# Load order at the start, w_out in long rows, and sixteen small loads late in the queue of a decode kernel

## Chip, cores, metric

One core of one Trainium2 chip at a time. The metric is device time in microseconds (us) of the whole kernel. Smaller is better.

## The reference, cut to what matters

A decode step for four sequences with one token each: an attention block over a cache of 4096 positions and 32 heads, and a gMLP block, both on the normalised input, added to the input.

```python
def _A_ref(x, k_cache, v_cache, wq, wo):             # x (4,1,640), caches (4,32,4096,128)
    q = (x @ wq).reshape(B, Sq, H, Dh).transpose(0, 2, 1, 3)
    scores = einsum('bhqd,bhkd->bhqk', q, k_cache) * Dh ** -0.5
    o = einsum('bhqk,bhkd->bhqd', softmax(scores), v_cache)
    return o.transpose(0, 2, 1, 3).reshape(B, Sq, H * Dh) @ wo

def _B_ref(x, w_in, w_sp, b_sp, w_out):              # w_in (640,1728), w_out (864,640)
    z = gelu(x @ w_in)
    z1, z2 = z[..., :864], layernorm(z[..., 864:])
    g = einsum('ts,bsf->btf', w_sp, z2) + b_sp       # S is 1: one scalar each
    return (z1 * g) @ w_out

xn = layernorm(x)
return x + _A_ref(xn, ...) + _B_ref(xn, ...)
```

The two caches are 268 MB in bfloat16 and every byte is used once.

## The kernel before

All large loads are issued on the queue of SyncE (SP), in program order. The K and V tiles (4 MB each), the weights of the start and the last wo share a pool of five buffers. Cuts are marked.

```python
wg = kv_tile("w_gmlp")                                       # buffer 0
nc.sync.dma_start(out=w_in,  in_=B_w_in.rearrange("(p c) f -> p c f", c=DC))
nc.sync.dma_start(out=w_out[:, 0:FC-1, :], in_=B_w_out[0:nf, :].rearrange("(c p) n -> p c n", p=P))  # rows of 1280 bytes
nc.sync.dma_start(out=w_out[:FL, FC-1, :], in_=B_w_out[nf:Fh, :])
for i, (c0, c1) in enumerate(((0, 3), (3, DC))):             # wq, two loads, buffers 1 and 2
    nc.sync.dma_start(out=..., in_=wq_v[:, c0:c1, :])
nc.scalar.dma_start(out=x_bf, in_=x_flat)
nc.scalar.dma_start(out=sb_bf[:, 0:1], in_=B_w_sp....to_broadcast((P, 1)))   # one 2-byte scalar to 128 partitions
nc.scalar.dma_start(out=sb_bf[:, 1:2], in_=B_b_sp.to_broadcast((P, 1)))
# ... layer norm of x, constants, gMLP, then q ...

def load_unit(cache, key, u, cuts=(0, T)):                   # a K or V tile
    t_sb = kv_tile(f"{key}{u}")
    for t0, t1 in zip(cuts[:-1], cuts[1:]):
        nc.sync.dma_start(out=t_sb[:, t0*Dh:t1*Dh], in_=src[:, t0*Dh:t1*Dh])

def load_x():                                                # x again, for the residual: 8 rows of 640 bytes
    nc.sync.dma_start(out=x_res[0:32:4, :], in_=x_flat.rearrange("b (h n) -> (b h) n", h=NH))

# in the schedule: load_x stands behind V30; then come V31 in four pieces and wo_last in three
at(NCH * (NU - 2) + VD, load_x)
```

The framework sets the semaphores. The trace shows how it does so for loads: eight semaphores are used in turn by all loads of SP and of ScalarE (ACT), and a load waits until the load eight places before it has landed. I call that the rule of eight. A load has landed when its last byte is in place and its semaphore says so.

## Time and profile before

| | before |
|---|---|
| time, median of 3 | 670.08 us |
| profiled execution | 670.88 us, span 669.1 us |
| bytes moved | 282.65 MB at 422 GB/s |
| busiest compute engine | TensorE, 50% of the span |
| time from 38 to 600 us | 431 GB/s, DMA share 1.00 |

In the views by stretches, each line has the stretch, its length, then busy time and number of instructions of each engine, the granted TensorE clock, the mean busy share of the 16 DMA engines, and GB/s. In the timelines of the SP queue each line has the start, the length from the first issue to the last of that group, line and operation, output and input, and the count. The time a sequencer waits between issues of a group is inside the length.

### The profile page before, as it was taken

The page shows a single profiled execution, that of the slowest core. Times are in us where ns is not written, and L with a number is a line of the kernel's source. Part 1 is how long each engine was busy: PE and PEld are TensorE (multiplying, and loading weights), DVE is VectorE, ACT ScalarE, POOL GpSimd, SP SyncE. Part 2 cuts the span into 40 slices and gives each one's busy share as a digit, 9 for nine tenths or more (in the row PEclk, how much of TensorE's full clock was granted, in tenths as well). Part 3 has the DMA queues.
Part 4 walks back from the last instruction along what each step waited for, and adds up shares of the span by engine and source line. Part 5 has one row for each costly group of instructions (what it writes and reads, how often), then busy time and mean ns, then how long its engine had stood idle before and what let it go on. Part 6 is the DMA issues. An engine that isn't in the chain of part 4 may idle for free.

```text
span 669.1 us, 6401 instructions
## 1 busy us (share of the span) xinstructions
PE 335.7 (50%) x2781; PEld 139.1 (21%) x2781; DVE 319.5 (48%) x253; ACT 60.4 (9%) x184; POOL 8.9 (1%) x40
## 2 busy tenths in 40 slices
PE   0647463546543664337555364454753366433745
PEld 0511121122111221113121031111311122111323
DVE  4279853465533455542555534346543355543300
ACT  0200210012000210003000030001200021000300
POOL 0010000000000000000000000000000000000000
PEclk9997777778777787676766677866767878567676
DMA  8999999999999999999999999999999999999995
GB/s 313 439 424 428 436 433 428 425 436 431 426 435 430 428 434 439 424 428 434 427 429 433 432 427 434 426 427 441 428 431 430 431 427 432 433 433 426 435 418 230
DMA packets 12900, 282.65 MB, mean 422 GB/s; under 512 B 1621, under 2 KB 3017, under 8 KB 4169
## 3 DMA queue, kind: packets, MB, share of 16 engines
q1 hardware_dynamic: 12568, 282.25, 98.6%
q8 instruction: 21, 0.34, 0.2%
q10 hardware_dynamic: 304, 0.01, 0.0%
q14 instruction: 7, 0.05, 0.0%
HBM read 282.25 MB, written 0.01 MB: 422 GB/s over the span
## 4 chain that ended last, share of the span: by engine, by line
DMA 56%; PE 15%; issue 13%; DVE 12%; ACT 3%; ACTq 0%; DVEq 0%
DMA k<-in_A_k_cache_dram 50%; DVE kT L318 8%; PE O L422 6%; DMA wo_last<-in_A_wo_dram 5%; PE S L336 3%; ACT p L364 3%; PE misc L439 2%; DMA sb_bf<-in_B_b_sp_dram 2%; PE x L377 1%; DVE m L343 1%; DVE om L442 1%; PE misc L251 1%; PE misc L347 1%; ACT O_sb L430 0%; PE zT_ps L209 0%
## 5 line engine op out<-in xcount | busy, mean ns | idle before, releaser
L318 DVE STREAM_TRANSPOSE kT<-k 128x2048 f32<-128x2048 f32 x128 | 284.6, 2280 | 215.0 <-DMA k<-in_A_k_cache_dram 212.4
L336 PE MATMUL S<-kT,QZ 128*32 128x512 bf16 x1024 | 203.7, 538 | 257.6 <-DVE kT L318 255.2
L336 PEld LDWEIGHTS <-QZ 128*32 128x32 bf16 x1024 | 57.3, 115 | 399.1 <-issue 386.7
L422 PE MATMUL O<-v,Zb 128*32 128x512 bf16 x992 | 93.1, 467 | 9.0 <-DMA v<-in_A_v_cache_dram 9.0
L422 PEld LDWEIGHTS <-Zb 128*32 128x32 bf16 x992 | 42.1, 112 | 41.0 <-issue 26.2
L364 ACT ACTIVATE p<-S,negmax 128x1024 bf16<-128x1024 f32 x16 | 17.7, 1109 | 272.0 <-DVE negmax L358 272.0
L430 ACT COPY O_sb<-O 128x512 f32<-128x512 f32 x16 | 9.4, 585 | 240.6 <-PE O L422 240.6
L388 ACT COPY Zb<-x 32x128 bf16<-32x128 bf16 x128 | 27.3, 255 | 10.2 <-PE x L377 9.5
L377 PE MATMUL x<-IdP,p 128*128 128x128 bf16 x128 | 16.1, 305 | 18.9 <-ACT p L364 18.6
L442 DVE SCALAR_TENSOR_TENSOR om<-misc,rinv,MkH 16x512 bf16<-16x512 f32 x7 | 5.2, 739 | 37.8 <-PE misc L439 37.8
L439 PE MATMUL misc<-O_sb,SelG 128*16 128x128 f32 x112 | 16.9, 289 | 2.0 <-DVE rinv L398 1.5
L377 PEld LDWEIGHTS <-p 128*128 128x128 bf16 x128 | 12.0, 138 | 22.6 <-ACT p L364 22.6
L275 POOL COPY QZ<-q 32x16 bf16<-32x16 bf16 x32 | 7.9, 246 | 455.4 <-PE S L336 420.9
L439 PEld LDWEIGHTS misc<-O_sb,SelG 128*16 128x16 f32 x112 | 10.1, 99 | 7.9 <-ACT O_sb L430 2.4
L474 DVE TENSOR_TENSOR oL<-misc,rinv 128x8 bf16<-128x8 f32 (+1 forms) x2 | 0.3, 168 | 22.6 <-PE misc L472 22.6
L343 DVE TENSOR_REDUCE m<-S 128x1 f32<-128x512 f32 x8 | 5.5, 691 | 10.2 <-PE S L336 10.2
L147 PE MATMUL misc<-ident_bf,wq 4*128 4x4 bf16 x5 | 0.4, 178 | 18.9 <-DVE wq L143 18.9
L368 DVE TENSOR_TENSOR rowsum<-rs 128x1 f32<-128x1 f32 x8 | 1.2, 155 | 17.0 <-ACT p L364 17.0
L347 PE MATMUL misc<-dg,ones_f 128*128 128x128 f32 x16 | 3.9, 324 | 9.0 <-DVE dg L345 9.0
L364 ACT ACT_TABLE_LOAD x1 | 1.3, 1283 | 54.8 <-DVE negmax L358 54.8
L460 PE MATMUL proj<-wo,oT 128*4 128x320 bf16 x56 | 5.0, 298 | 1.9 <-DVE oT L453 1.9
L251 PE MATMUL misc<-xnT,wq 128*128 128x4 bf16 x160 | 4.7, 166 | 1.1 <-issue 0.8
(93 smaller groups left out, 75.9 us busy)
## 6 DMA issues: line engine op xcount, KB each, us to landing
k<-in_A_k_cache_dram SPq DMA_DIRECT2D x32, 4096.0 KB, 43.3
v<-in_A_v_cache_dram SPq DMA_DIRECT2D x31, 4096.0 KB, 41.1
wo<-in_A_wo_dram SPq DMA_DIRECT2D x7, 640.0 KB, 44.6
wq<-in_A_wq_dram SPq DMA_DIRECT2D x1, 3072.0 KB, 19.5
w_gmlp<-in_B_w_in_dram SPq DMA_DIRECT2D x1, 2160.0 KB, 9.3
wq<-in_A_wq_dram SPq DMA_DIRECT2D x1, 2048.0 KB
v<-in_A_v_cache_dram SPq DMA_DIRECT2D x1, 2048.0 KB
v<-in_A_v_cache_dram SPq DMA_DIRECT2D x1, 1024.0 KB, 38.4
```

The source lines that it names most:

```text
L251: nc.tensor.matmul(q_ps[:, h, :], lhsT=wq_t[c][:, h * Dh:(h + 1) * Dh], rhs=xnT[:, c, :], start=(c == 0), stop=(c == DC - 1))
L318: nc.vector.transpose(kT[:], kw[:, ch * n:(ch + 1) * n])
L336: nc.tensor.matmul(S_ps[32 * q:32 * q + 32, :, :], lhsT=qz[:, b, kw, w0:w0 + 32], rhs=kT[:, i, :, kw // 2, :, kw % 2], start=(b == 0 and c ...
L343: nc.vector.tensor_reduce(out=m1[:], in_=S_ps[:].rearrange("p k m -> p (k m)"), axis=AX.X, op=ALU.max)
L347: nc.tensor.matmul(mm[:], lhsT=ones_f[:], rhs=dg[:], start=True, stop=True)
L364: nc.scalar.activation(out=p_i[:], in_=S_ps[:, 8 * i:8 * i + 8, None, :].to_broadcast((P, 8, HG, M)), func=ACT.Exp, bias=negmax[:, 0:1], s ...
L377: nc.tensor.transpose(x[:, t, :], p_bf[t // 8][:, t % 8].rearrange("p h m -> p (h m)"), IdP[:])
L388: nc.scalar.copy(out=dst, in_=src[:, 2 * bb + b1])
L422: nc.tensor.matmul(O_ps[32 * q:32 * q + 32, :, :], lhsT=Zb[bb][:, w0:w0 + 32], rhs=vv[:, e // 16, e % 16, :, :], start=(b1 == 0 and e < 4) ...
L430: nc.scalar.copy(out=O_sb[:], in_=O_ps[:])
L439: nc.tensor.matmul(oh[:], lhsT=SelG[:, bb, c].rearrange("p h b -> p (h b)"), rhs=O_sb[:, c, :], start=(bb == 0 and c == 0), stop=(bb == 1 ...
L442: nc.vector.scalar_tensor_tensor(out=om[:], in0=oh[:, None, :].to_broadcast((G, HG, Dh)), scalar=state.pop(("rinv", g))[:, 0:1], in1=MkH[: ...
```

## The change

The intent: let q, which the first K tile needs, come first; let the gMLP weights follow with w_out in long rows; take the two scalar loads off the ACT queue. Sixteen small loads over 1 to 16 rows are issued behind `load_x`, into a tile that nothing reads.

```diff
-    (w_gmlp: w_in, w_out, w_out rest on nc.sync)        # first before, moved behind wq
     (wq, two loads on nc.sync; x on nc.scalar)
-    nc.scalar.dma_start(out=sb_bf[:, 0:1], in_=B_w_sp....to_broadcast((P, 1)))
-    nc.scalar.dma_start(out=sb_bf[:, 1:2], in_=B_b_sp.to_broadcast((P, 1)))
+    nc.gpsimd.dma_start(out=sb_bf[:, 0:1], in_=B_w_sp....to_broadcast((P, 1)))
+    nc.gpsimd.dma_start(out=sb_bf[:, 1:2], in_=B_b_sp.to_broadcast((P, 1)))
+    (w_gmlp here, with:)
-    ... in_=B_w_out[0:nf, :].rearrange("(c p) n -> p c n", p=P)
+    ... in_=B_w_out[0:nf, :].rearrange("(p c) n -> p c n", p=P)      # one row of 7680 bytes a partition
...
+    (q matmuls and q3, moved ahead of the gMLP)
-    nc.tensor.matmul(zT_ps[...], lhsT=w_in[:, c, f0:f0 + n], ...)
+    w = w_in[:, c, f0:f0 + nf].rearrange("p (f a) -> p a f", a=FC - 1)[:, fc, :]   # strided, to match w_out
-    nc.vector.tensor_copy(out=sb_f[:], in_=sb_bf[:])
+    nc.gpsimd.tensor_copy(out=sb_f[:], in_=sb_bf[:])
...
+    probe = const.tile([64, 264], BF16)
+    def load_probe():
+        c0 = 0
+        for k in range(1, 17):
+            n = 8 + k
+            nc.sync.dma_start(out=probe[0:4 * k:4, c0:c0 + n], in_=A_wo[0:k, 0:n])
+            c0 += n
...
-    at(NCH * (NU - 2) + VD, load_x)
+    at(NCH * (NU - 2) + VD, lambda: (load_x(), load_probe()))
```

More of the change, by code (lines that the diff above doesn't have):

```diff
@@ L90 @@
     out_flat = out.rearrange("b s d -> (b s) d")
-    wg = kv_tile("w_gmlp")
-    n_in = DC * F2
-    w_in = wg[:, 0:n_in].rearrange("p (c f) -> p c f", c=DC)
-    nc.sync.dma_start(out=w_in, in_=B_w_in.rearrange("(p c) f -> p c f", c=DC))
-    w_out = wg[:, n_in:n_in + FC * NOUT].rearrange("p (c n) -> p c n", c=FC)
-    nf = (FC - 1) * P
-    nc.sync.dma_start(out=w_out[:, 0:FC - 1, :], in_=B_w_out[0:nf, :].rearrange("(c p) n -> p c n", p=P))
-    nc.sync.dma_start(out=w_out[:FL, FC - 1, :], in_=B_w_out[nf:Fh, :])
     wq_v = A_wq.rearrange("(p c) n -> p c n", c=DC)
@@ L113 @@
     sb_bf = const.tile([P, 2], BF16)
-    nc.scalar.dma_start(out=sb_bf[:, 0:1], in_=B_w_sp.rearrange("a b -> (a b)").to_broadcast((P, 1)))
-    nc.scalar.dma_start(out=sb_bf[:, 1:2], in_=B_b_sp.to_broadcast((P, 1)))
+    nc.gpsimd.dma_start(out=sb_bf[:, 0:1], in_=B_w_sp.rearrange("a b -> (a b)").to_broadcast((P, 1)))
+    nc.gpsimd.dma_start(out=sb_bf[:, 1:2], in_=B_b_sp.to_broadcast((P, 1)))
     sb_f = const.tile([P, 2], F32)
+    wg = kv_tile("w_gmlp")
+    n_in = DC * F2
+    w_in = wg[:, 0:n_in].rearrange("p (c f) -> p c f", c=DC)
+    nc.sync.dma_start(out=w_in, in_=B_w_in.rearrange("(p c) f -> p c f", c=DC))
+    w_out = wg[:, n_in:n_in + FC * NOUT].rearrange("p (c n) -> p c n", c=FC)
+    nf = (FC - 1) * P
+    nc.sync.dma_start(out=w_out[:, 0:FC - 1, :], in_=B_w_out[0:nf, :].rearrange("(p c) n -> p c n", p=P))
+    nc.sync.dma_start(out=w_out[:FL, FC - 1, :], in_=B_w_out[nf:Fh, :])
     ident_bf = const.tile([P, P], BF16)
@@ L200 @@
     proj = ps_j.tile([64, 512], F32)
+    q_ps = misc_ps([P, H, B], F32)
+    for h in range(H):
+        for c in range(DC):
+            nc.tensor.matmul(q_ps[:, h, :], lhsT=wq_t[c][:, h * Dh:(h + 1) * Dh], rhs=xnT[:, c, :],
+                             start=(c == 0), stop=(c == DC - 1))
+    q_bf = const.tile([P, H * B], BF16)
+    nc.vector.tensor_copy(out=q_bf[:], in_=q_ps[:].rearrange("p h b -> p (h b)"))
+    q3_ps = misc_ps([P, 4, H * B], F32)
+    for kw in range(4):
+        nc.tensor.matmul(q3_ps[:, kw, :], lhsT=Pm[:, kw, :, :].rearrange("p a j -> p (a j)"), rhs=q_bf[:],
+                         start=True, stop=True)
+    q3 = const.tile([P, 4, H * B], BF16)
+    nc.vector.tensor_copy(out=q3[:], in_=q3_ps[:])
     zT_ps = ps_g.tile([P, 2, FC, B], F32)
@@ L206 @@
             n = P if fc < FC - 1 else FL
-            f0 = part * Fh + fc * P
+            f0 = part * Fh
             for c in range(DC):
-                nc.tensor.matmul(zT_ps[:n, part, fc, :], lhsT=w_in[:, c, f0:f0 + n],
+                if fc < FC - 1:
+                    w = w_in[:, c, f0:f0 + nf].rearrange("p (f a) -> p a f", a=FC - 1)[:, fc, :]
+                else:
+                    w = w_in[:, c, f0 + nf:f0 + Fh]
+                nc.tensor.matmul(zT_ps[:n, part, fc, :], lhsT=w,
                                  rhs=xnT[:, c, :], start=(c == 0), stop=(c == DC - 1))
@@ L245 @@
     nc.vector.tensor_tensor(out=uT[:, :, 0:B], in0=z1, in1=t1[:], op=ALU.mult)
-    q_ps = misc_ps([P, H, B], F32)
-    for h in range(H):
-        for c in range(DC):
-            nc.tensor.matmul(q_ps[:, h, :], lhsT=wq_t[c][:, h * Dh:(h + 1) * Dh], rhs=xnT[:, c, :],
-                             start=(c == 0), stop=(c == DC - 1))
-    q_bf = const.tile([P, H * B], BF16)
-    nc.vector.tensor_copy(out=q_bf[:], in_=q_ps[:].rearrange("p h b -> p (h b)"))
-    q3_ps = misc_ps([P, 4, H * B], F32)
-    for kw in range(4):
-        nc.tensor.matmul(q3_ps[:, kw, :], lhsT=Pm[:, kw, :, :].rearrange("p a j -> p (a j)"), rhs=q_bf[:],
-                         start=True, stop=True)
-    q3 = const.tile([P, 4, H * B], BF16)
-    nc.vector.tensor_copy(out=q3[:], in_=q3_ps[:])
     for fc in range(FC):
```

## The prediction

> **What bounds the kernel now.** I read the page first: the busy table, the slices, the chain of waits.
>
> ```profile
> PE 335.7 (50%) x2781; PEld 139.1 (21%) x2781; DVE 319.5 (48%) x253; ACT 60.4 (9%) x184; POOL 8.9 (1%) x40
> ...
> DMA  8999999999999999999999999999999999999995
> GB/s 313 439 424 428 436 433 428 425 436 431 426 435 430 428 434 439 424 428 434 427 429 433 432 427 434 426 427 441 428 431 430 431 427 432 433 433 426 435 418 230
> ...
> DMA 56%; PE 15%; issue 13%; DVE 12%; ACT 3%; ACTq 0%; DVEq 0%
> ```
>
> No compute engine is busy over half of the span, and the transfer engines are full in every slice but the first and the last. The kernel streams 282 MB, so the time is start + bytes at full rate + tail. The issues view says how deep the queue is:
>
> ```profile
> k<-in_A_k_cache_dram SPq DMA_DIRECT2D x32, 4096.0 KB, 43.3
> v<-in_A_v_cache_dram SPq DMA_DIRECT2D x31, 4096.0 KB, 41.1
> wo<-in_A_wo_dram SPq DMA_DIRECT2D x7, 640.0 KB, 44.6
> ```
>
> A 4 MB load lands 41 to 43 us after its issue, although it takes only 4.194 MB / 431 GB/s = 9.7 us to move. Four loads are queued ahead of it: the sequencer is always far ahead, and that margin is what must not be lost. Next, busy time by stretches (the last two columns are DMA share and GB/s):
>
> ```profile
> 2.00:3.00 1.00, 0.00 (x0) 0.00 (x0) 0.92 (x1) 0.01 (x1) 0.00 (x0) 1.00 0.21 69
> 3.00:7.00 4.00, 0.00 (x0) 0.00 (x0) 1.11 (x3) 1.27 (x1) 0.00 (x0) 1.00 0.99 397
> 7.00:11.00 4.00, 0.00 (x0) 0.00 (x0) 0.00 (x0) 0.00 (x0) 0.00 (x0) 1.00 0.72 236
> 11.00:25.00 14.00, 3.75 (x80) 3.48 (x80) 7.95 (x37) 3.43 (x6) 0.00 (x0) 1.00 1.06 436
> ...
> 37.90:600.00 562.10, 287.05 (x2114) 110.17 (x2116) 290.67 (x184) 48.27 (x154) 5.89 (x24) 0.73 1.00 431
> ```
>
> The steady rate is 431 GB/s. The only recoverable hole at the start is 7 to 11 us: 236 GB/s, while w_out (in 1280-byte rows) and the two broadcast scalars go through. Last, the timeline of the issuing queue at the end and the queue's own waits:
>
> ```profile
> 603.30 3.16 SPq L289 DMA_DIRECT2D v<-in_A_v_cache_dram  x2
> 606.52 0.78 SPq L307 DMA_DIRECT2D x_res<-in_A_x_dram  x1
> 622.75 2.59 SPq L289 DMA_DIRECT2D v<-in_A_v_cache_dram  x4
> 634.78 19.70 SPq L299 DMA_DIRECT2D wo_last<-in_A_wo_dram  x3
> ```
> ```profile
> SPq L299 <- DMA v<-in_A_v_cache_dram: 28.0, 3, 9.4
> ```
>
> The three wo_last loads are issued at 634.78, 644.43 and 654.15. They go to one buffer that is free from the start of that stretch, and yet the last two wait for V loads that they have nothing to do with. The records behind the view name the semaphore of each transfer: eight of them are used in turn over all SP and ACT loads, and a load waits until the load eight places earlier has landed. Eight before the third wo_last is V30, which landed at 654.14; eight before the second is V29, at 644.42. That rule costs nothing now. It decides this case.
>
> **What the Trainium skill says.** "DMA: Bandwidth & Descriptors", section "Anatomy of one DMA — SWDGE (gpsimd) path": semaphore waits happen on the issuing sequencer, and the transfer engines just consume their queues. So a waiting issue holds all later ones of that queue; the wo_last issues above agree. The same page, section "Why a DMA increments its semaphore by 16 and not by 1", asks for one semaphore per transfer in flight (the reason for the rule of eight) and says that a transfer over k rows, k up to 16, uses k engines. The trace agrees as far as it can: each 4-row store at the end left 4 data packets and 4 semaphore packets. The same page, section "Rules for kernel authors": transfers under 64 KB pay mostly overhead, and transfers should be coalesced. The trace has 55 to 60 ns for a 1280-byte packet against 1218 ns for 32768 bytes (47.6 ns for 1280).
>
> **The change part by part.**
>
> *Order of the weights, w_out in long rows, scalars on the software queue.* The bytes stay. w_out goes from 864 packets of 1280 bytes (54 per engine, 59 ns each) to 8 of 7680 and 6 of 1280 per engine: saved 48 x (59 - 47.6) ns = 0.55 us. Its descriptors are also fewer, so the hole at 7 to 11 us, worth 4 x (431 - 236) / 431 = 1.8 us and containing part of that 0.55, should nearly close. The loss before 3 us (first packet at 1.76 us, then slow first packets) stays[...]. The 256 two-byte packets still run on the same engines, now beside wq. I count a gain of 2.0 us (1 to 3).
>
> Is it on the path? Yes: from 11 us on the engines never run dry, so bytes moved earlier shift every later landing. Compute at the start lies beside it: wq lands near 14.5 us (5.24 MB at 431 GB/s from 1.8, plus receipt), the 160 q matmuls take 4.7 us, QZ is full near 23 us against 37.1 now, and w_gmlp lands near 23 with some 8 us of gMLP behind it. The first K tile lands near 36 (37.9 now), so nothing there is late. The strided weight loads of zT may be slower than the 2.5 us of now; they have 5 us of room. K2 to K4 wait for q and gMLP, but five loads are in the queue up to about 40 us.
>
> *Sixteen small loads.* They carry 2 x sum of k(8 + k) = 5.2 KB, nothing in bandwidth. They stand after x_res and before V31 and wo_last. With numbers by place: K31, wo6, V27, V28, V29, V30, x, then p1 to p16, then V31 in four pieces, then three wo_last. By the rule of eight, p1 waits for V26, p2 K31, p3 wo6, p4 V27, p5 V28, p6 V29 and **p7 for V30**. V31 comes behind p16 on the same in-order queue, so it cannot be issued before V30, the last load in the queue, has landed. Now it is issued at 622.75, 31 us ahead. The queue runs dry at V30.
>
> What it costs, counted on the slowest engine, whose last V30 packet ends at 653.67 (landing 654.14, 0.47 us later):
> - landing to p7: 0.47 us;
> - ten issues, p7 to p16. A bare issue takes 0.33 us, the 8-row x_res behind another load took 0.78, the 4-row x load on ACT 0.99. I take 0.55 plus the 0.05 between neighbours: 6.0 us. p15 waits for p7's landing and p16 for p8's, but eight issues (4.8 us) exceed the 2 us that I allow for a small load on an idle queue;
> - V31's issue to first packet: 1.0 us (0.73 to 1.76 at the start, 0.78 for the output stores);
> - slow first packets after an idle stretch: 0.5 us.
>
> Sum 8.0 us. Then V31 and wo_last take what they take now, 653.67 to 665.3, and the tail after them is the same. Faster engines, which start V31 from 647.6 now, lose their lead, but they do not set the end.
>
> Net: 670.1 - 2.0 + 8.0 = **676.0 us**, 0.9% slower.
>
> **The rivals.** (1) *The semaphores do not bind*, or the small loads fit into the 31 us of slack: then only the start counts, about 668. For it: the queue is 40 us deep. Against it: the wo_last waits, to the hundredth of a microsecond. (2) *The small loads are serialised one after another* because they write one tile: fifteen round trips of 2 us, some 30 us, near 698. Against it: the pieces of w_gmlp, of sb_bf and of V31 are issued without such waits. (3) *Issues are cheap*, 0.35 to 0.4 us: bubble 5.5 to 6, about 673.5. Or dear, 0.8 to 0.85: bubble 10 to 10.5, about 678.5. This is what I know least. (4) *The start gives nothing*, as the two-byte packets and the software queue cause the hole: 678. (5) Instruction fetches of 16 KB, 21 in the trace, hold one engine for about 1.06 us each; one in the tail, where all engines now restart together, adds 1.
>
> **Range and chances.** Gain 1 to 3, bubble 5.5 to 10.5, with a microsecond for a fetch: 672 to 681; I widen the lower end for a bubble of 4: 671.0 to 681.0. Over 2% slower means above 683.5, which only serialisation reaches (6%). Over 2% faster means under 656.7: the start has not that much to give (1%). Within 2%: 93%.
>
> **What would show it.** Right: V31 is issued after V30 has landed, near 660 instead of 622.75; the queue's waits show small loads waiting for V loads, the longest near 9 us; the GB/s in the slices near the end drop and the last slice fills; wo_last is issued in one run, not 9.7 us apart; the first K tile lands near 36. Wrong: V31 still issued near 622 (rival 1), or gaps of about 2 us between the small issues (rival 2). The duration of each small issue tells the size of the bubble, and the landing of the first K tile the gain at the start.

## The result and the profile after

| | before | after |
|---|---|---|
| median, same chip | 670.25 us (4 runs) | 681.22 us (4 runs, 681.17 to 681.79) |
| ratio | | 1.0164, 95% interval 1.0147 to 1.0182 |
| profiled execution | 670.88 us, span 669.1 us | 681.23 us, span 679.2 us |

Ratios here and below are the mean time of one kernel's runs over the mean of the other's of the same rounds, so they are not quite the ratio of the medians quoted. The change cost 11.0 us by the medians: it is slower, and just outside the range of the prediction (671 to 681).

The page of the kernel after, its slices, its DMA queues and its chain:

```profile
DMA  8999999999999999999999999999999999999927
GB/s 332 424 432 430 432 432 429 428 431 429 426 432 429 430 432 429 430 429 429 430 432 428 433 429 430 431 428 431 430 427 430 432 432 431 432 418 435 430 117 287
...
q0 software_dynamic: 64, 0.00, 0.0%
q10 hardware_dynamic: 16, 0.01, 0.0%
...
DMA 62%; PE 12%; issue 12%; DVE 10%; ACT 3%; SPq 1%; DVEq 0%; ACTq 0%
```

Slice 39 of 40 fell from 418 to 117 GB/s: a hole of some 10 us just before the end, which the kernel before does not have. The first slice rose only from 313 to 332. The scalars are now on queue q0. "SPq" is new in the chain: the issuing sequencer itself is now on the path.

The timeline of the SP queue after, late part (L294 is a K or V load, L312 x_res, L320 the small loads, L304 wo_last):

```profile
602.33 3.17 SPq L294 DMA_DIRECT2D v<-in_A_v_cache_dram  x2
605.55 0.80 SPq L312 DMA_DIRECT2D x_res<-in_A_x_dram  x1
606.40 54.95 SPq L320 DMA_DIRECT2D probe<-in_A_wo_dram  x16
661.47 2.03 SPq L294 DMA_DIRECT2D v<-in_A_v_cache_dram  x4
663.59 1.40 SPq L304 DMA_DIRECT2D wo_last<-in_A_wo_dram  x3
```

V31 is issued at 661.47; it was 622.75 before. The sixteen small loads occupy the queue for 55 us, and nothing that comes after them can pass. What they wait for, from the queue's own waits (us in total, times, longest):

```profile
SPq L320 <- DMA v<-in_A_v_cache_dram: 36.1, 4, 9.1
...
SPq L320 <- DMA k<-in_A_k_cache_dram: 6.4, 1, 6.4
...
SPq L320 <- DMA wo<-in_A_wo_dram: 0.9, 1, 0.9
```

One K load, one wo load, four V loads: these are the waits of the second to the seventh small load by the rule of eight. By the issue records the seventh starts at 653.66, 0.02 us after V30 has landed (653.64). From there ten small issues follow each other with 0.04 us between, in the stretch from 653.66 to V31's issue:

```profile
653.66 7.70 SPq L320 DMA_DIRECT2D probe<-in_A_wo_dram  x10
```

And the DMA engines in the stretches that this cuts out, first after, then before:

```profile
653.20:662.60 9.40, 5.84 (x42) 2.98 (x42) 0.17 (x1) 0.58 (x1) 0.00 (x0) 0.50 0.03 4
662.60:675.30 12.70, 4.47 (x132) 3.98 (x133) 0.17 (x1) 0.00 (x0) 0.00 (x0) 0.50 0.98 381
```
```profile
653.70:665.30 11.60, 8.79 (x174) 6.02 (x175) 0.34 (x2) 0.58 (x1) 0.00 (x0) 0.65 0.71 280
```

The stretches are cut by the packet records. Before, the slowest engine ends its last V30 packet at 653.67 and the last wo_last packet ends at 665.29, 11.62 us later, with no pause. After, the last V30 packet ends at 653.19; then the engines stand at 4 GB/s until 662.60, and the rest ends at 675.23. So the tail is 22.04 us in place of 11.62. The spans differ by 10.1 us: 10.4 in this tail, 0.5 less before it (V30 lands earlier) and 0.2 behind it. The 10.4 us more are made of:

| piece | forecast | measured |
|---|---|---|
| last V30 packet to the seventh small issue | 0.47 | 0.47 (653.19 to 653.66) |
| ten small issues | 6.0 | 7.8 (653.66 to 661.47) |
| V31's issue to its first packet | 1.0 | 1.1 (661.47 to 662.60) |
| longer transfer from there (12.63 against 11.62) | 0.5 | 1.0 |
| sum | 8.0 | 10.4 |

The last piece is the cold restart: the first 16 KB packet of each engine took about 1350 ns in place of 613. That is 0.7 of the 1.0; the rest is not taken apart.

At the start, the stretches of before and then of after:

```profile
6.00:8.00 2.00, 0.00 (x0) 0.00 (x0) 0.00 (x0) 0.00 (x0) 0.00 (x0) 1.00 0.95 337
8.00:11.00 3.00, 0.00 (x0) 0.00 (x0) 0.00 (x0) 0.00 (x0) 0.00 (x0) 1.00 0.68 216
```
```profile
6.00:8.00 2.00, 0.00 (x0) 0.00 (x0) 1.94 (x6) 0.48 (x2) 0.00 (x0) 1.00 0.51 184
8.00:11.00 3.00, 0.35 (x5) 0.27 (x5) 2.21 (x17) 1.09 (x1) 0.00 (x0) 1.00 0.99 415
```

The hole was not closed. It moved from 8 to 11 us, where w_out had gone through, to 6 to 8 us, where wq goes through in rows of 24 KB. So a hole can stand without short rows; whether they made the one of before is tested by e10 and e11. The first K tile is ready earlier (the first transpose starts at 36.34, before at 37.91), but V30 lands only 0.5 us earlier (653.64 against 654.14).

### The profile page after: what moved, and what is told of

The parts are those of the page before. It is cut to its first block, busy times and chain, and to the rows that moved or that the text cites. A ratio compares the mean times of both kernels' runs of the same rounds, so it can differ in the third digit from the quotient of the medians.

```text
span 679.2 us, 6419 instructions
## 1 busy us (share of the span) xinstructions
PE 334.2 (49%) x2781; PEld 140.5 (21%) x2781; DVE 318.8 (47%) x252; ACT 60.4 (9%) x184; POOL 10.7 (2%) x43
## 4 chain that ended last, share of the span: by engine, by line
DMA 62%; PE 12%; issue 12%; DVE 10%; ACT 3%; SPq 1%; DVEq 0%; ACTq 0%
DMA k<-in_A_k_cache_dram 51%; DMA v<-in_A_v_cache_dram 7%; DVE kT L332 7%; PE O L436 5%; PE S L350 3%; DMA wq<-in_A_wq_dram 2%; ACT p L378 2%; DMA wo_last<-in_A_wo_dram 2%; PE x L391 1%; PE misc L453 1%; SPq L320 1%; DVE m L357 1%; PE misc L207 1%; DVE om L456 1%; PE misc L361 1%
## 5 line engine op out<-in xcount | busy, mean ns | idle before, releaser
L436 PE MATMUL O<-v,Zb 128*32 128x512 bf16 x992 | 90.1, 457 | 9.3 <-DMA v<-in_A_v_cache_dram 9.3
L402 ACT COPY Zb<-x 32x128 bf16<-32x128 bf16 x128 | 27.3, 254 | 10.1 <-PE x L391 9.4
L548 PE MATMUL ol<-Zb,v 128*128 128x4 bf16 x128 | 4.0, 167 | 10.7 <-DMA v<-in_A_v_cache_dram 10.7
L207 PEld LDWEIGHTS <-wq 128*128 128x128 bf16 x160 | 4.4, 104 | 7.9 <-DMA wq<-in_A_wq_dram 7.9
```

Of the source, the lines that this page charges most:

```text
L207: nc.tensor.matmul(q_ps[:, h, :], lhsT=wq_t[c][:, h * Dh:(h + 1) * Dh], rhs=xnT[:, c, :], start=(c == 0), stop=(c == DC - 1))
L402: nc.scalar.copy(out=dst, in_=src[:, 2 * bb + b1])
L436: nc.tensor.matmul(O_ps[32 * q:32 * q + 32, :, :], lhsT=Zb[bb][:, w0:w0 + 32], rhs=vv[:, e // 16, e % 16, :, :], start=(b1 == 0 and e < 4) ...
```

## The experiments

Theory W: the rule of eight makes V31 wait behind ten issues that start when V30 has landed, so the queue runs dry; 10.4 us. Its rivals: the slowdown is the start's, or each small load has a price of its own wherever it stands (C). Theory H for the start: the 256 two-byte packets of the scalars make the hole, on whichever queue; its rival D: the hole is a cold queue (one that has just begun to move data) or a late supply of descriptors (the entries that tell an engine what to move).

Twelve kernels ran, in three groups, each with the kernel before on the same chip.

| run | median us | before, same rounds | ratio, 95% |
|---|---|---|---|
| e1, no small loads | 670.42 | 670.66 | 1.0003 (0.9990 to 1.0015) |
| e2, before with small loads | 681.75 | 670.66 | 1.0172 (1.0158 to 1.0186) |
| e3, e1 with no scalar loads | 668.46 | 670.66 | 0.9973 (0.9960 to 0.9985) |
| e4, e1 with scalars on SP, behind the weights | 669.28 | 670.66 | 0.9985 (0.9972 to 0.9997) |
| e5, three small loads | 670.96 | 670.23 | 1.0012 (0.9997 to 1.0027) |
| e6, six small loads | 675.31 | 670.23 | 1.0076 (1.0059 to 1.0093) |
| e7, sixteen loads of 16 rows | 680.39 | 670.23 | 1.0155 (1.0140 to 1.0170) |
| e8, small loads on the software queue | 671.21 | 670.23 | 1.0017 (1.0002 to 1.0032) |
| e9, e1 with scalars as one element each | 669.03 | 669.99 | 0.9983 (0.9969 to 0.9996) |
| e10, e3 with short rows of w_out | 668.88 | 669.99 | 0.9980 (0.9968 to 0.9993) |
| e11, before with no scalar loads | 668.78 | 669.99 | 0.9980 (0.9968 to 0.9993) |
| e12, small loads spread over sixteen V loads | 670.81 | 669.99 | 1.0010 (0.9996 to 1.0024) |

The kernel before itself comes in two levels in two of the three groups, near 669.7 and near 670.8. Differences under about 0.7 us between groups are therefore not read from the times.

A second small difference goes with the kernel. Between 40 and 600 us the mean packet of 32 KB took 1218.2 to 1218.4 ns in the profiled runs of before, e1, e3, e4, e10 and e11, and 1219.3 to 1219.4 ns in those of after, e2, e5 to e9 and e12. At 504 such packets for each engine that is 0.5 us. Every kernel with the tile of the small loads is in the slower set, in all three groups, and so is e9, which has no such tile. Why is not known, and there is one profile of each kernel.

### e1: the change without the small loads

```diff
-    at(NCH * (NU - 2) + VD, lambda: (load_x(), load_probe()))
+    at(NCH * (NU - 2) + VD, load_x)
```

> The changed kernel without the sixteen small loads. Theory W (the rule of eight makes V31 wait behind ten issues after V30 has landed; dry stretch 10.4 us by the trace): V31 is issued near 622 again and the time falls by about 10.4 us from the changed kernel, to some 0.5 to 1.0 us below the kernel before of the same rounds (what the start has brought). Rival (the slowdown comes from the start or from the software queue): it stays 8 us or more above the kernel before.

The SP queue of e1, late part:

```profile
605.58 0.78 SPq L312 DMA_DIRECT2D x_res<-in_A_x_dram  x1
621.80 2.61 SPq L294 DMA_DIRECT2D v<-in_A_v_cache_dram  x4
633.83 19.72 SPq L304 DMA_DIRECT2D wo_last<-in_A_wo_dram  x3
```

V31 is issued at 621.80 again, and the time is that of the kernel before. The whole loss is the small loads'. The start has brought nothing that the times can show (0.2 us by the medians, the interval holds 1).

### e2: the kernel before with the small loads

```diff
+    probe = const.tile([64, 264], BF16)        # and load_probe as in the change
-    at(NCH * (NU - 2) + VD, load_x)
+    at(NCH * (NU - 2) + VD, lambda: (load_x(), load_probe()))
```

> The kernel before with the sixteen small loads and nothing else. Theory W: 10.4 us above the kernel before of the same rounds (10 to 11), V30 landing as in the kernel before and V31 issued 7.8 us after it. Rival (start of the change to blame): within 1 us of the kernel before.

```profile
607.42 54.44 SPq L315 DMA_DIRECT2D probe<-in_A_wo_dram  x16
661.97 2.03 SPq L289 DMA_DIRECT2D v<-in_A_v_cache_dram  x4
```

11.1 us by the medians, so slightly over the 10 to 11 expected. The seventh small issue starts at 654.16 and V31 follows 7.8 us later, as in the changed kernel. e1 and e2 together (1.0003 x 1.0172 = 1.0175) make the whole change within the intervals.

### e5 and e6: three and six small loads

```diff
-        for k in range(1, 17):
+        for k in range(1, 4):        # e6: range(1, 7)
```

> The changed kernel with 3 small loads in place of 16. Theory W counts places: eight before the four pieces of V31 stand V27, V28, V29 and V30, so only the last piece waits for V30, with 3.7 MB of V31 still queued ahead of it. No dry stretch; within 0.5 us of e1 and of the kernel before (0 to +0.5 us). Rival C (each small load costs its own issue time or transfer time, whatever its place): 3/16 of 11 us, that is 2 us above the kernel before.

> The changed kernel with 6 small loads. Theory W: eight before the first piece of V31 stands V30, so V31 is issued when V30 has landed, with no small issue between: landing 0.47 + issue to first packet 1.2 + slow first packets 0.8, that is 2.4 us above the kernel before (2 to 3). Rival C: 6/16 of 11 us, 4.1 us above.

The SP queue of e5, then of e6:

```profile
606.51 8.58 SPq L320 DMA_DIRECT2D probe<-in_A_wo_dram  x3
624.16 29.50 SPq L294 DMA_DIRECT2D v<-in_A_v_cache_dram  x4
653.75 1.37 SPq L304 DMA_DIRECT2D wo_last<-in_A_wo_dram  x3
```
```profile
607.29 37.73 SPq L320 DMA_DIRECT2D probe<-in_A_wo_dram  x6
654.08 1.88 SPq L294 DMA_DIRECT2D v<-in_A_v_cache_dram  x4
656.05 1.44 SPq L304 DMA_DIRECT2D wo_last<-in_A_wo_dram  x3
```

In e5 the four pieces of V31 are issued over 29.5 us, the last when V30 has landed, and the packet records show no pause (last V30 packet to last packet 11.70 us against 11.62 before). The time is 0.7 us above the kernel before, 0.2 more than expected. C wanted 2. In e6 the first piece of V31 waits for V30, as counted.

But e6 is 5.1 us above the kernel before, where W had said 2.4 and C 4.1. The time alone would have favoured C; the records do not. From the last V30 packet (653.57) to V31's first packet (655.06) are 1.49 us, and fifteen of the sixteen engines are done by 667.8, which is 2.6 us more than the 11.62 of before. The sixteenth runs until 669.21. The queues in the transfer stretch of e6 (packets, MB, share):

```profile
q1 hardware_dynamic: 1132, 4.78, 86.6%
q8 instruction: 1, 0.02, 0.4%
```

One instruction fetch fell into the transfer here; its packet took about 1 us of one engine. In the changed kernel the fetch came at 658.91, in the dry stretch, where it cost nothing. In the kernel before and in e5 one fell into the transfer too (661.75 and 661.17), and their tails were 11.62 and 11.70; there the engines had not restarted together. That the late engine of e6 is the one with the fetch is my reading of the records, not a run of its own. That makes 2.6 + 1.4 = 4.0. Against e5 of the same rounds, which has the same start and no dry stretch, e6 is 4.4 us slower, so little is left open.

### e7: sixteen loads of sixteen rows

```diff
-            nc.sync.dma_start(out=probe[0:4 * k:4, c0:c0 + n], in_=A_wo[0:k, 0:n])
+            nc.sync.dma_start(out=probe[0:64:4, c0:c0 + n], in_=A_wo[0:16, 0:n])
```

> The changed kernel with all sixteen small loads over 16 rows (16 engines), so ten issues after V30 as before. In the changed kernel the issue over 16 rows took 0.58 us and those over 7 to 15 rows 0.67 to 0.80. If the issue time goes with the engines left out: ten times about 0.15 less, 1.2 to 1.8 us below the changed kernel, about 9.5 us above the kernel before. If every small load costs the same issue and 0.58 was chance: within 0.3 us of the changed kernel (11 above).

All small issues of the changed kernel, then of e7 (duration in ns: least, median, most):

```profile
L320 SPq DMA_DIRECT2D probe<-in_A_wo_dram x16: 363/713/802, 606.4 to 660.8; - x16
```
```profile
L320 SPq DMA_DIRECT2D probe<-in_A_wo_dram x16: 492/587/597, 606.6 to 659.2; - x16
```

More rows made each issue cheaper: 0.59 us over 16 engines in place of 0.67 to 0.80 over 7 to 15. The ten issues took 6.3 us in place of 7.8. The time came out 10.2 us above the kernel before, where 9.5 was expected, and 9.4 above e5 of the same rounds. The times alone do not tell e7 from the changed kernel (1.0155 and 1.0164, with intervals that overlap); the records do. The tail from the last V30 packet is 21.06 us in place of 22.04, so 1.0 of the 1.5 us came through: the first issue of V31 took 0.84 us here in place of 0.51. So the duration of the issue is on the path. That the engines left out lengthen it, as I expected, does not follow: in the changed kernel one row took 0.36 us, with fifteen engines left out, two to six rows took 0.61 to 0.71, fifteen rows 0.80 and sixteen 0.58.

### e8 and e12: the same loads elsewhere

```diff
-            nc.sync.dma_start(out=probe[0:4 * k:4, ...        # e8
+            nc.gpsimd.dma_start(out=probe[0:4 * k:4, ...
-    at(NCH * (NU - 2) + VD, lambda: (load_x(), load_probe()))  # e12
+    at(NCH * (NU - 2) + VD, load_x)
+    for k in range(1, 17):
+        at(NCH * (NU - 2 - k) + VD, lambda k=k: load_probe(k))
```

> The changed kernel with the sixteen small loads issued on the software queue. Theory W: they neither stand before V31 on the SP queue nor take places in its turn of eight semaphores; V31 is issued near 622 and the time is that of e1, within 0.5 us of the kernel before. Rival (the sixteen transfers themselves hold the engines or the tail): still several us above.

> The changed kernel with the same sixteen small loads, one behind each of sixteen V loads of the steady part in place of all in a row. Theory W: eight places now hold four large and four small loads, so each wait is for a load that has landed or is about to, the queue never runs dry; within 1 us of the kernel before. Rival C (each small load costs about 0.65 us wherever it stands): 10 us above.

The SP queue of e8, then of e12:

```profile
622.34 2.58 SPq L294 DMA_DIRECT2D v<-in_A_v_cache_dram  x4
634.37 19.74 SPq L304 DMA_DIRECT2D wo_last<-in_A_wo_dram  x3
```
```profile
583.79 0.71 SPq L319 DMA_DIRECT2D probe<-in_A_wo_dram  x1
586.02 0.34 SPq L294 DMA_DIRECT2D v<-in_A_v_cache_dram  x1
593.51 0.61 SPq L319 DMA_DIRECT2D probe<-in_A_wo_dram  x1
603.28 0.33 SPq L294 DMA_DIRECT2D v<-in_A_v_cache_dram  x1
```

Both move the same sixteen loads and both are within about 1 us of the kernel before. e8 is 1.0 above it, twice the 0.5 expected, and its interval does not reach 1; e5 of the same rounds is 0.7 above, and 0.5 of either can be the slower packets told above. e12 is 0.8 above. In e8 the loads left the SP queue but also the tail: with nothing to wait for, they were issued between 13.0 and 26.7 us. So e8 shows that V31 is free without them, and not what sixteen transfers beside the tail would cost. In e12 an issue takes 0.75 us in the median (0.28 to 0.96), as ever, but other loads lie in the queue meanwhile. C is out: issues of equal length cost 10 us in a row behind the last load and 0.8 us or less when spread. V31 is issued at 624.31 in e12, 1.6 us later than in the kernel before, and still far ahead of V30's landing.

### e3, e11: no scalar loads

```diff
-    nc.gpsimd.dma_start(out=sb_bf[:, 0:1], in_=B_w_sp....to_broadcast((P, 1)))   # e11: the nc.scalar lines
-    nc.gpsimd.dma_start(out=sb_bf[:, 1:2], in_=B_b_sp.to_broadcast((P, 1)))
+    nc.gpsimd.memset(sb_bf[:, 0:1], 0.0)
+    nc.gpsimd.memset(sb_bf[:, 1:2], 1.0)
```

> As e1, and the two scalar loads replaced by constants (a wrong result on purpose: the gate gets 0 and 1 in place of the true scalars). Theory H (the two-byte packets of the scalars, on whichever queue, cause the hole in which the engines move under 300 GB/s between 6 and 8 us): the hole closes and it is 1.2 to 2 us below e1. Rival D (the hole is a cold queue or a late supply of descriptors after the fourth packet of an engine): the hole stays, and it is within 0.3 us of e1.

> The kernel before with the scalar loads replaced by constants (a wrong result on purpose). Theory H: the hole at 7 to 11 us was the scalars' too, and 1.3 to 1.9 us are gained here already; what is left to e3 is the row length, 0.5 us. Rival (in the kernel before the hole came from the short rows of w_out and the order): the hole stays, less than 0.5 us gained.

Both compute a wrong gate; the error is too small for the comparison with the reference to mind. The stretches of e1, then e3, then e11:

```profile
6.00:8.00 2.00, 0.00 (x0) 0.00 (x0) 1.94 (x6) 0.48 (x2) 0.00 (x0) 1.00 0.33 111
```
```profile
6.00:8.00 2.00, 0.00 (x0) 0.00 (x0) 1.94 (x6) 0.48 (x2) 0.00 (x0) 1.00 1.00 430
```
```profile
6.00:8.00 2.00, 0.00 (x0) 0.00 (x0) 1.90 (x8) 0.00 (x0) 0.00 (x0) 1.00 0.87 365
8.00:11.00 3.00, 0.00 (x0) 0.00 (x0) 2.53 (x5) 0.85 (x2) 0.00 (x0) 1.00 1.30 445
```

111 GB/s became 430 when the scalar loads went, and nothing else was changed: 2.0 us of time between e1 and e3, which ran in the same rounds. In the kernel before, 216 GB/s became 445 (a share above 1 comes of counting a packet in the stretch in which it starts), and 1.2 us were gained. The scalar loads make the hole in both kernels. D is out: the queue is as cold in e3. "Two-byte packets" was too narrow, though: the ACT queue of the kernel before records 256 packets of 2 bytes, the software queue of after and e1 only 32 of 16 bytes and 32 semaphore packets of 4. All of these 64 together last 0.8 us, spread over 16 engines; the time goes in the pauses before and between them.

"DMA: Bandwidth & Descriptors" of the Trainium skill says in its "Specifications" that below 512 bytes the engine does a read-modify-write, and under "Queues, rings and completion order" that an engine takes turns between the queues that it has work for. Both fit, but neither is shown to be the cause. e4 below has the scalars on the queue of the weights, with no queues to alternate between, and still pays 0.8 us. What stops the engines no run here shows by itself.

### e4 and e9: the scalars in another way

```diff
     # e4: the two loads unchanged, but nc.sync and behind the weights
     # e9: one element each, spread by a matmul with ones
-    nc.gpsimd.dma_start(out=sb_bf[:, 0:1], in_=B_w_sp....to_broadcast((P, 1)))
+    nc.gpsimd.dma_start(out=sb_1[:, 0:1], in_=B_w_sp)
...
+    nc.tensor.matmul(sb_ps[:], lhsT=ones_f[0:1, :], rhs=sb_1f[:], start=True, stop=True)
+    nc.vector.tensor_copy(out=sb_f[:], in_=sb_ps[:])
```

> As e1, with the scalars at the end of the weights on the SP queue, correct result. Theory H in the form that the packets of two queues taking turns cause the hole: no hole at 6 to 8 us, a small one near 23, and 1 to 2 us below e1. If the two-byte packets cost the same wherever they run: the hole moves to 23 us and the time is that of e1. Rival D: hole at 6 to 8 us stays.

> e1 (no small loads) with each scalar loaded as one element and spread over the partitions by a matmul with ones, correct result. Theory H (256 two-byte packets cause the hole): the hole at 6 to 8 us closes as in e3; 1.7 to 2.2 us below the kernel before, the best of all. Rival (any use of the software queue beside the SP queue stops the engines): the hole stays, and it is within 0.5 us of the kernel before.

The stretch of e9:

```profile
6.00:8.00 2.00, 0.00 (x0) 0.00 (x0) 1.94 (x6) 0.48 (x2) 0.00 (x0) 1.00 1.04 442
```

e9 still uses the software queue for two loads, and the hole is gone. So it is the 128-fold broadcast that makes the hole, and not the use of this queue by itself. By the packet records the mean over the engines of the first K packet's start is 24.9 us before, 24.5 in e1, 22.8 in e3 and 22.8 in e9: the same start for e9 as without any scalars. In time e9 gained 1.0 us by the medians, less than the 1.7 to 2.2 expected. Its 32 KB packets were 0.9 ns slower than those of e3 in the profiled runs, 504 of them on each engine, which is 0.4 us; the rest stays open. e4 gained 1.1 over e1, at the lower end of what was expected: on one queue with the weights the broadcast still costs 0.8 us against e3 (the first K packet at 23.9), and the records show pauses of one to two microseconds on most engines near 23.

e9 loads the true scalars and beats both kernels: 0.17% below before, 1.8% below the change (0.9983 against 1.0164, from different groups). It is not a 2% gain. That it is correct follows from its edit; the comparison with the reference, which also lets the wrong gate of e3 pass, does not test it.

### e10: short rows of w_out

```diff
-    ... in_=B_w_out[0:nf, :].rearrange("(p c) n -> p c n", p=P)       # from e3
+    ... in_=B_w_out[0:nf, :].rearrange("(c p) n -> p c n", p=P)
```

> e3 (no small loads, no scalar loads, a wrong result on purpose) with w_out in 1280-byte rows again. By the packet times of the prediction, long rows save 48 x (59 - 47.6) ns = 0.55 us on each engine: e10 0.4 to 0.7 us above e3, about 1.5 below the kernel before. Rival (the hole of the kernel before came from the short rows): 1.5 us or more above e3, and a hole where w_out goes through.

0.4 us above e3 by the medians, in another group; the first K packet starts at 23.1 on average against 22.8. That agrees in size with the 0.55 of the prediction and is not sharp enough to say more. No hole appears where w_out goes through. e10 and e11 differ in the order of the weights, and of q and the gMLP, and in the engine of one small copy, and their times are the same (668.88 and 668.78): the order is worth nothing that the times show.

## Why the prediction was wrong, point by point

**What bounds the kernel:** right. Every change of the time by more than 1 us goes with a gap in the DMA stream.

**The rule of eight and its place:** right, to the load. "p7 for V30" is what the trace shows, and V31 came at 661.5 where "near 660" was said. The signs named at the end of the prediction came true: waits of up to 9.1 us for V loads, a drop in the GB/s near the end, wo_last in one run.

**The cost of the sixteen loads, 8.0 us:** the term that failed is "I take 0.55 plus the 0.05 between neighbours: 6.0 us". The ten issues took 7.8. The prediction had three samples, 0.33 for a bare issue, 0.78 for x_res and 0.99 for x, and took a middle. The ten averaged 0.73 plus 0.05. The nearest sample was x_res, the one that was like them: a load over few rows directly behind another load. The cold restart was 1.0 in place of 0.5. Together these two are 2.3 of the 2.4 us that the sum was short.

**The gain at the start, 2.0 us:** the step that failed is "the hole at 7 to 11 us ... should nearly close". I gave the hole to the short rows of w_out because they were in it; the scalars were in it too, and the change only moved them to another queue. e1 shows a gain of about zero, e3 and e11 show whose the hole was. The small part that was worked out from packet times, 0.55 us for the rows, is of the size that e10 shows.

**The rivals:** serialisation (2) is out, the small issues are 0.04 us apart. (3), dear issues, and (4), a start that gives nothing, both came true. I had priced each alone, at 678.5 and 678. Both at once make 670.1 - 0 + 10.5 = 680.6, close to the 681.2 measured. The forecast of 676.0 was short by 5.2 us: 2.0 of the start, 2.4 of the bubble, and 0.8 that the times and traces here do not settle. Rival (5), a fetch among engines that restart together, did not meet the changed kernel (658.91, in the dry stretch) and may be what e6 paid.

**A sign that misled:** "the landing of the first K tile" was to tell the gain at the start. It came 1.6 us earlier (1.1 in e1) and the time did not follow. A tile lands when the slowest engine is done. In the kernel before an instruction fetch held an engine from 35.73 to 36.79 us, and the last engine's semaphore packet of that tile came at 36.78, when the other fifteen had been through by 36.15; by the records it stood behind the fetch. The mean over the engines, 24.9 against 24.3 us at the first K packet, was the better measure.

## What to carry to other kernels

Count loads in flight, not bytes: where a fixed number of semaphores goes round, a row of tiny loads uses up places that large loads would have filled, and the load behind them waits for the last large one to land. Spread such loads among the large ones or put them on another queue, and look for two-byte broadcasts in every start-up: one element and a matmul with ones did the same here without the hole (e9). When a hole in the stream holds two suspects, take each out before giving the hole to one of them.

## What the Trainium skill lacked or had wrong

- "DMA: Bandwidth & Descriptors", "Issuing engines are not separate DMA queues", calls the sequencer's issue time usually small against the DMA. Here ten issues with an empty queue behind them were 7.8 of the 10.4 us lost.
- The same page, on how many engines a load uses: it gives no issue time by that number. In these runs a load over 7 to 15 rows behind another took 0.67 to 0.80 us to issue, over 16 rows 0.58 to 0.60, over one row 0.36, a K or V load on its own 0.33.
- The same page, "Specifications", has about 0.6 us to the first byte on this path. From V31's issue to its first packet 1.1 us passed (1.0 in e6), and each engine's first 16 KB packet then took about 1.35 us in place of 0.61.
- The same page has the limit of 512 bytes but no price of a scalar broadcast to 128 partitions. Two of them, 512 bytes in all, cost 2.0 us on the software queue (e1 against e3) and about 1.2 on the ACT queue (e11 against before).
- "Runtime: NRT & Kernel Launch", "Instruction fetch mechanics", calls the cost of a 16 KiB block mostly hidden. The 21 or 22 fetches of a run each held one of the 16 DMA engines for about 1.07 us on average; in e6, where one fell among engines that had restarted together, one engine ended 1.4 us after the rest.
- No page that I read has the rule of eight, which here decided the result: a load waits for the landing of the load eight places before.
